# Another order for the 703 steps of a fused retention and channel-mix kernel

## Chip, cores and metric

The kernel runs on one core of a Trainium2 chip. The metric is the time of the device in microseconds (us), median of three runs. TensorE multiplies, VectorE (DVE in the rows), ScalarE (ACT) and GpSimd (POOL) work on whole tiles, SyncE (SP) starts most DMAs. PEld in the rows is TensorE loading weights, PE its multiplying.

## What is computed

Four sequences of 768 tokens go through a retention layer with 8 heads of 64 numbers (worked in blocks of 64 tokens with a state that is carried from block to block), and its output through a gated channel mix of width 512 and inner width 1024. All is f32.

```python
for b in range(nb):                      # blocks of 64 tokens
    intra = einsum(qb, kb) * Dmask       # decayed scores inside the block
    intra = einsum(intra, vb)
    inter = einsum(qb * lam_pow, kv_state)
    out[:, :, sl] = intra + inter
    kv_state = lam_block * kv_state + einsum(kb * rev_pow, vb)
x_prev = x shifted by one token
xk = mu_k * x + (1 - mu_k) * x_prev
xr = mu_r * x + (1 - mu_r) * x_prev
k = maximum(xk @ w_k, 0)
v = k * k @ w_v
return sigmoid(xr @ w_r) * v
```

## The kernel before

The tokens are worked in six rounds, n = 0 to 5, of 128 tokens (two blocks) of each sequence; the heads in four pairs, hp = 0 to 3. A round first does the retention of its four pairs, then the gate, then the two products of the channel mix. To keep f32 accuracy an f32 operand is split into a high and a low part (`split`, line 161: a copy on ScalarE, a subtraction on VectorE), and a product is three passes of matmuls, high by high, high by low, low by high (`product`, line 390).

What the kernel does is cut into steps of one letter and two digits; in most the first digit is the round. The step functions are:

- L, N, H (lines 104 to 118): loads by SyncE. S (176) loads a part of the weights; c (200), C (204) and D (221) turn it into high and low parts: a cast on ScalarE, a bit operation on VectorE, and a split. In these the letter r, k or v says of which weight.
- A `scores` (251), on TensorE: 16 small f32 matmuls for one head pair, which the trace records as 32. a `decay` (268), on VectorE, multiplies them by the decay mask. q (279) and k (283) scale queries on VectorE and keys on ScalarE, k with two instructions.
- U `sums` (289), on TensorE: 16 small matmuls (32 records) that give the two sums for a pair's state. u and w `next_state` (306), on VectorE from round 1 on: u makes the state after the first block from the sum, w the state after the second one from the sum and what u wrote. In round 0 u is a copy on ScalarE. Two pairs (0 and 1, 2 and 3) share the two PSUM tiles of the sums, each one half of both.
- B `values` (331) and G `values_too` (351), on TensorE, for two pairs at once: 16 and 48 small matmuls (32 and 96 records). g `turn` (348) copies one element on VectorE into a tile named junk, and so ties G to the end of B.
- e, E `mix_prev` (367): ScalarE scales the output of a pair, GpSimd moves the last column; f, F `mix` (374): VectorE adds the other term; y, x `split_x` (382): the split for the product. Small letters are for k, capitals for the gate in e and f.
- R, Q `r_part` (405): the gate's product, two of four output tiles each, 12 large matmuls from round 1 on; s (412) its sigmoid on ScalarE. K `k_part` (416): one of eight tiles of the first product, 12 large matmuls; h (422) squares its positive part (ScalarE, and VectorE from round 1 on), p (433) splits two tiles of it. V `v_part` (438): half of one tile of the second product, 12 large matmuls; o (460) multiplies by the gate on VectorE (the tile is called rt) and starts the DMA out from ScalarE's queue.
- Z `keep_busy` (156): matmuls on zeros at the start.

A step of TensorE that writes PSUM takes one of four buffers of the pool `ps_m` (tiles rp, kp, vp, xp), the one buffer of the scores, or the two of the sums. It waits until the readers of what was there are done.

The order of all steps is a table of text, `ORDER` (line 495), 703 steps long. The program calls them one after another (lines 472 to 477), and every engine keeps its own instructions in that order (`InOrder`, line 25). So an engine that waits in one step holds up all its later steps.

```python
for step in ORDER.split():
    ...
        i, j = step[1], int(step[2])
        steps[step[0]](i if i in "rkv" else int(i), j)
```

Of the kernel before, what the change touches and what calls it, by code (L numbers as in the profile page):

```python
# [492 lines left out]


ORDER = """
L01 M00 L00 Z10 d01 N01 A01 a01 H01 d02 H00 L02 k01 d00 A00 H02 U01 a00 N00 B01 L03 d03 A02 k00 u01 E01 l00 a02 H03
U00 k02 l02 u00 N02 B00 k03 N03 Sr0 A03 e00 E00 F01 U02 a03 Sr1 Sr2 U03 Sr3 Sk1 u02 u03 cr0 Sk0 e01 B03 E03 cr1 F00
B02 Cr0 f00 L11 Cr1 f01 cr2 L10 E02 R00 Cr2 F03 cr3 Q00 Q01 F02 y00 Dr2 N10 R01 Cr3 x02 e02 Q02 l01 N11 R02 x03 y01
Sk3 Dr3 Q03 N12 R03 f02 ck1 A10 ck0 e03 Ck0 L12 k11 k10 Ck1 f03 y02 Dk0 Dk1 U10 A11 U11 s00 y03 a10 s01 ck3 s02 Sk2
a11 q11 K03 h03 k12 u11 u10 q10 K01 h01 B10 g10 ck2 Sv1 Ck3 Sv0 Ck2 Dk3 A12 G10 s03 Dk2 N13 L13 cv1 K00 Sv3 a12 cv0  # L500
h00 w11 K02 h02 K07 Cv1 K06 l03 E10 Cv0 w10 e10 e11 Sv2 F10 U12 Dv0 E11 f11 f10 k13 p00 F11 p01 h07 A13 U13 q12 q13
K05 K04 cv3 Dv1 cv2 h05 Cv3 L21 a13 V00 Cv2 u13 h06 Dv3 N21 N23 h04 u12 Dv2 V02 B12 g12 A21 p02 y10 p03 G12 V01 x11
o00 x10 L20 e13 V03 y11 V04 e12 q21 N20 E12 o01 F12 f13 f12 a21 V06 V05 Dr0 o02 w12 y12 w13 L23 y13 V07 k20 A20 U20
K10 u20 E13 F13 K11 x12 a20 L22 k21 h10 K16 o03 Q10 x13 Q11 q20 h11 h16 Q12 Q13 U21 B20 A23 u21 N22 g20 A22 G20 p10
s12 k23 s13 N31 K17 h17 E21 K12 N30 q23 F21 e20 e21 a22 h12 p13 K14 f21 L30 k30 w21 K15 w20 E20 f20 h15 a23 h14 K13
k22 h13 F20 R10 x20 U23 L31 U22 B22 R11 u23 R12 g22 y21 u22 p11 q22 R13 G22 w22 o53 w23 A31 y20 A30 k31 q30 U30 E23
U31 s11 e23 e22 N33 s10 V10 a30 x21 E22 F23 L33 f22 F22 y22 f23 a31 V16 V14 p12 V17 u31 x23 V11 o10 V12 V15 x22 y23
u30 V13 o11 o12 N32 K27 o13 K26 Q20 Q21 h27 Q22 h26 Q23 p23 s22 q31 L32 B30 g30 A32 A33 G30 e31 s23 E30 f31 K24 K25
E31 e30 L41 F31 h24 K20 h20 N41 a33 q33 f30 w31 K23 w30 K21 h25 L40 F30 q32 K22 p22 h21 k32 R20 R21 k33 a32 h22 U33
k40 x30 h23 U32 y31 B32 N40 u32 R22 p20 R23 w32 y30 g32 u33 p21 G32 w33 A40 s20 A41 a41 k41 E32 U41 q41 F32 e33 e32  # L510
f33 x32 U40 q40 f32 V20 V21 u40 V22 a40 N43 N42 L42 o20 E33 s21 k42 y33 V23 B40 u41 y32 F33 g40 A42 w41 L43 x31 x33
A43 G40 o21 E41 E40 N50 Q30 e40 Q31 N51 a43 e41 F41 F40 f40 L50 Q32 Q33 s33 q42 K32 f41 V24 V25 s32 k43 K31 h32 V26
a42 K33 V27 h31 h33 K30 w40 L51 h30 K37 o22 k50 p31 R30 R31 q43 R32 R33 x40 o23 U42 h37 s31 U43 u42 u43 B42 g42 A50
A51 G42 s30 L52 q51 K34 K35 p30 h34 K36 a50 h35 E42 y41 y40 e42 a51 L53 h36 F42 e43 V32 V34 f42 f43 q50 x42 w42 p33
V30 p32 V31 y42 x41 y43 V35 o30 V33 E43 N52 o31 N53 V36 k52 V37 F43 K41 K42 o32 k51 w43 U50 x43 o33 u51 B50 g50 u50
A52 h41 A53 G50 h42 E51 a52 K43 e50 F51 h43 e51 K40 a53 E50 f50 K47 p41 F50 f51 K44 K45 h40 p40 h47 K46 h45 h46 R40
q52 R41 h44 k53 p42 R42 R43 B52 U52 u53 g52 s41 q53 s40 Q40 Q41 u52 Q42 Q43 G52 y51 s42 e53 y50 f53 s43 x50 e52 f52
p43 V42 V40 V41 x51 E52 E53 F53 o40 F52 y53 x52 y52 V43 K52 K53 V44 h53 K51 V45 o41 K54 o42 h52 V46 x53 h54 V47 p51
o43 K50 h51 Q50 K55 Q51 h50 h55 Q52 Q53 R50 s53 p50 K57 R51 s52 R52 h57 K56 h56 V52 R53 V50 p52 p53 V51 s50 V56 o50
s51 V53 V54 V55 o51 o52 V57  # L520
"""


# [60 lines left out]
```

## Time and profile before

| | before |
|---|---|
| median of 3 runs | 395.51 us (395.47 to 395.63) |
| span of the profiled execution | 393.7 us |
| TensorE multiplying | 386.9 us, 98% of the span |
| TensorE loading weights | 317.5 us |
| VectorE | 208.8 us |
| ScalarE | 168.5 us |
| GpSimd | 23.5 us |

The profile was taken in one execution, whose span runs from the first to the last instruction. All work is recorded through one helper, so every instruction stands at line 33 (L33), and groups are told apart by their tiles: `sc` the scores, `u` the sums, `st` the state, `mv` (in round 0 `mw`) the decayed scores, `xp` the output of the retention, `ts` the mix, `xh` and `xl` its two parts, `rp`, `kp` and `vp` the three products, `wst` a weight as it was loaded. TensorE's matmuls overlap one another, and their printed ends have the pipeline in them: what two rows tell of the time that one takes is the distance between their starts.

### The profile page before, as it was taken

Reading aid. Unit: us, or ns where it says so; the run is one execution under the profiler, and the core shown is the slowest. Engines: PE = TensorE matmul, PEld = TensorE weight load, DVE = VectorE, ACT = ScalarE, POOL = GpSimd, SP = SyncE. Lnnn points to the kernel's source line nnn. Section 1 sums busy time; section 2 is a strip of 40 time slices with the busy share of each in tenths; the row PEclk is TensorE's granted clock in tenths of the full one; section 3 lists DMA queues with packets and bytes.
Section 4 is the critical chain, followed back from the end, with each engine's and each line's share of the span. In section 5 each row is a group of like instructions: output and inputs, shape, how many; then the busy total and the mean of one; then the engine's idle time right before and its main releaser. Section 6 shows DMA issues by size and latency. Waiting matters only on the chain.

```text
span 393.7 us, 9414 instructions
## 1 busy us (share of the span) xinstructions
PE 386.9 (98%) x4154; PEld 317.5 (81%) x4154; DVE 208.8 (53%) x322; ACT 168.5 (43%) x276; POOL 23.5 (6%) x97
## 2 busy tenths in 40 slices
PE   7999999999999999999999999999999999999996
PEld 3757888888888888888888888888888888888885
DVE  4898989763377723358754026573373272232311
ACT  2798999443365412418353023542243360222300
POOL 2121010200001100100110000100000000000000
PEclk9999999999999999999999999999999999999999
DMA  7999861810320502230525001501000000000011
GB/s 265 412 407 412 305 246 55 303 45 28 116 102 11 208 27 82 81 136 2 200 68 219 0 27 42 203 19 64 28 2 1 3 27 27 28 27 0 2 42 65
DMA packets 15560, 42.64 MB, mean 108 GB/s; under 512 B 1440, under 2 KB 1824, under 8 KB 15520
## 3 DMA queue, kind: packets, MB, share of 16 engines
q1 hardware_dynamic: 11920, 35.76, 24.6%
q10 hardware_dynamic: 3600, 6.29, 4.4%
q8 instruction: 32, 0.52, 0.5%
q14 instruction: 8, 0.07, 0.1%
HBM read 35.76 MB, written 6.29 MB: 107 GB/s over the span
## 4 chain that ended last, share of the span: by engine, by line
PE 84%; ACT 8%; DMA 4%; DVE 1%; issue 1%; SPq 1%; POOL 0%; ACTq 0%; POOLq 0%
PE vp L33 32%; PE kp L33 29%; PE rp L33 14%; PE xp L33 4%; DMA wst<-w_r 2%; ACT kf L33 2%; ACT top L33 2%; PE u L33 2%; PE sc L33 2%; DMA in<-first 2%; ACT hiv L33 1%; ACT hik L33 1%; ACT ts L33 1%; SPq L33 1%; ACT xh L33 1%
## 5 line engine op out<-in xcount | busy, mean ns | idle before, releaser
L33 PE MATMUL vp<-hiv,k 128*128 128x512 f32 (+1 forms) x400 | 121.8, 382 | 0.0
L33 PEld LDWEIGHTS vp<-hiv,k 128*128 128x128 f32 x400 | 74.1, 188 | 14.6
L33 PE MATMUL vp<-lov,k 128*128 128x512 f32 (+1 forms) x200 | 76.1, 381 | 0.0
L33 PE MATMUL kp<-xh,hik 128*128 128x512 f32 x192 | 75.6, 394 | 0.3 <-ACT rt L33 0.3
L33 PE MATMUL kp<-xl,hik 128*128 128x512 f32 x192 | 74.8, 390 | 0.0
L33 PE MATMUL kp<-xh,lok 128*128 128x512 f32 x192 | 74.8, 390 | 0.0
L33 ACT ACTIVATE kf<-kp 128x512 f32<-128x512 f32 x48 | 28.3, 595 | 99.3 <-PE kp L33 84.1
L33 DVE TENSOR_TENSOR kf<-kp,kf 128x512 f32<-128x512 f32 x40 | 27.5, 690 | 67.7 <-ACT kf L33 67.6
L33 ACT ACTIVATE ts<-xp,omu 128x512 f32<-128x512 f32 x48 | 31.3, 687 | 29.8 <-DVE rt L33 12.1
L33 PEld LDWEIGHTS vp<-lov,k 128*128 128x128 f32 x200 | 37.6, 188 | 7.1
L33 PEld LDWEIGHTS kp<-xh,hik 128*128 128x128 f32 x192 | 36.0, 188 | 8.5 <-ACT rt L33 0.5
L33 PEld LDWEIGHTS kp<-xh,lok 128*128 128x128 f32 x192 | 36.0, 188 | 7.6
L33 PEld LDWEIGHTS kp<-xl,hik 128*128 128x128 f32 x192 | 36.0, 188 | 7.2
L33 DVE TENSOR_TENSOR xl<-ts,xh 128x512 fp32r<-128x512 f32 x46 | 30.9, 687 | 19.3 <-ACT xh L33 19.3
L33 DVE TENSOR_TENSOR rt<-vp,rt 128x512 f32<-128x512 f32 (+1 forms) x25 | 16.4, 666 | 45.4 <-PE vp L33 43.6
L33 ACT CAST xh<-ts 128x512 fp32r<-128x512 f32 x46 | 27.3, 617 | 25.2 <-DVE rt L33 20.3
L33 DVE SCALAR_TENSOR_TENSOR ts<-xp,mus,ts 128x512 f32<-128x512 f32 x46 | 33.4, 746 | 8.5 <-ACT ts L33 5.5
L33 DVE TENSOR_TENSOR k<-kf,k 128x1024 fp32r<-128x1024 f32 x24 | 29.2, 1222 | 13.0 <-ACT k L33 12.8
L33 PE MATMUL rp<-hir,xh 128*128 128x512 f32 x88 | 35.1, 399 | 0.0
L33 PE MATMUL rp<-hir,xl 128*128 128x512 f32 x88 | 34.3, 390 | 0.0
L33 PE MATMUL rp<-lor,xh 128*128 128x512 f32 x88 | 34.3, 389 | 0.0
L33 ACT CAST k<-kf 128x1024 fp32r<-128x1024 f32 x24 | 24.8, 1048 | 9.4 <-DVE kf L33 7.5
(58 smaller groups left out, 354.3 us busy)
## 6 DMA issues: line engine op xcount, KB each, us to landing
in<-kk SPq DMA_DIRECT2D x20, 512.0 KB, 6.4
in<-qv SPq DMA_DIRECT2D x20, 512.0 KB, 5.5
out<-rt ACTq DMA_DIRECT2D x23, 256.0 KB, 2.0
wst<-w_k SPq DMA_DIRECT2D x4, 1023.8 KB, 12.8
wst<-w_v SPq DMA_DIRECT2D x4, 1023.8 KB, 9.5
in<-first SPq DMA_DIRECT2D x4, 512.0 KB, 5.9
in<-first SPq DMA_DIRECT2D x8, 256.0 KB, 6.6
wst<-w_r SPq DMA_DIRECT2D x4, 511.8 KB, 8.8
```

Of the source, the lines that this page charges most:

```text
L33: return lambda *args, **kw: self.tc.keep_in_program_order(op(*args, **kw))
```

## The change

The 703 steps are the same ones, and no other line is touched. The table is written in another order from its first step to its last; some of its rows, of before and of after:

```diff
 ORDER = """
-L01 M00 L00 Z10 d01 N01 A01 a01 H01 d02 H00 L02 k01 d00 A00 H02 U01 a00 N00 B01 L03 d03 A02 k00 u01 E01 l00 a02 H03
-U00 k02 l02 u00 N02 B00 k03 N03 Sr0 A03 e00 E00 F01 U02 a03 Sr1 Sr2 U03 Sr3 Sk1 u02 u03 cr0 Sk0 e01 B03 E03 cr1 F00
...
-k22 h13 F20 R10 x20 U23 L31 U22 B22 R11 u23 R12 g22 y21 u22 p11 q22 R13 G22 w22 o53 w23 A31 y20 A30 k31 q30 U30 E23
...
+Z10 L01 N01 M00 d01 L00 A01 H01 l01 N02 a01 A00 H00 d00 k01 U01 L02 l02 N00 H03 L03 a00 k00 B01 E01 u01 d03 H02 A02 e01
+d02 k03 B00 a02 U00 u00 k02 f01 E00 N03 A03 Sr0 U02 U03 Sr1 F01 a03 B03 Sr2 F00 Sr3 Sk0 u02 u03 cr0 e00 Cr0 y01 E03 cr1
...
+Q10 o11 y21 V16 Q11 Q12 Q13 o10 w20 V17 x20 a22 U23 a23 u23 w23 A30 U22 u22 s13 B22 s12 g22 o13 A31 k31 G22 q31 e23 w22
+x21 L32 V14 e22 E23 V15 F23 x23 f23 E22 Q20 Q21 L33 F22 x22 f22 y22 Q22 y23 Q23 K21 s22 U30 N32 s23 a30 N33 h21 U31 u31
+K22 a31 w31 u30 B30 q30 g30 A32 h22 G30 w30 e30 k32 E30 e31 L41 A33 f30 a33 k33 o12 E31 K20 F30 k41 K25 q33 f31 F31 N41
+a32 R20 q32 N40 R21 h20 R22 R23 p20 x30 s20 x31 L40 U33 B32 s21 U32 u33 A40 u32 A41 g32 G32 K23 N43 h25 h23 q41 a41 K24
...
+V27 f32 y32 o22 o20 K30 q40 A43 B40 k43 U40 o23 g40 u40 U41 A42 u41 x33 G40 E40 K31 h30 K32 a42 x32 E41 h31 L51 h32 k42
...
```

Some places show what this does to single engines. The first is ScalarE at the start, in round 0: `in` are the scalings of keys (k, two rows for one step), `st` the copies u, `ts` the steps e and E, `top` the cast of the first weight part. Before:

```order
L33 ACTIVATE in<-in,Dw 128x4x64 x4
L33 COPY st<-u 128x256
L33 ACTIVATE ts<-xp,omu 128x4x128
L33 ACTIVATE in<-in,Dw 128x4x64 x2
L33 COPY st<-u 128x256
L33 ACTIVATE in<-in,Dw 128x4x64 x2
L33 ACTIVATE ts<-xp,omu 128x4x128 x2
L33 COPY st<-u 128x256 x2
L33 CAST top_100<-wst 128x512
```

After:

```order
L33 ACTIVATE in<-in,Dw 128x4x64 x4
L33 ACTIVATE ts<-xp,omu 128x4x128
L33 COPY st<-u 128x256
L33 ACTIVATE ts<-xp,omu 128x4x128
L33 ACTIVATE in<-in,Dw 128x4x64 x2
L33 COPY st<-u 128x256
L33 ACTIVATE in<-in,Dw 128x4x64 x2
L33 ACTIVATE ts<-xp,omu 128x4x128
L33 COPY st<-u 128x256 x2
L33 CAST top_100<-wst 128x512
```

Two more steps of mixing stand ahead of the cast where one stood in between, and one of them moved ahead of the copy.

The second is TensorE in round 2 where the sums of pairs 3 and 2 are made: U23 and U22 are 16 small matmuls each. Before, U23 is the first row of `u` here, U22 the next four, and B22 follows:

```order
L33 MATMUL rp<-hir_1091,xh_1013 128x512 [waits DVE_49]
L33 MATMUL rp<-lor_1093,xh_1013 128x512
L33 MATMUL rp<-hir_1091,xl_84 128x512
L33 MATMUL u<-in 64x64 x16
L33 MATMUL u<-in 64x64 [waits Activation_49]
L33 MATMUL u<-in 64x64
L33 MATMUL u<-in 64x64 [waits Activation_49]
L33 MATMUL u<-in 64x64 x13
L33 MATMUL xp<-mv,in 64x64 [waits DVE_49] x2
```

After, A30 (`sc`) stands between U23 and U22, B22 (`xp`) behind:

```order
L33 MATMUL vp<-hiv_989,k_3_993 128x512 x2
L33 MATMUL vp<-lov_990,k_3_993 128x512
L33 MATMUL vp<-hiv_989,k_3_993 128x512
L33 MATMUL u<-in 64x64 [waits DVE_49]
L33 MATMUL u<-in 64x64 x15
L33 MATMUL sc<-in 64x64 [waits DMAHW7_49,DMAHW5_49,DVE_49]
L33 MATMUL sc<-in 64x64 x15
L33 MATMUL u<-in 64x64 [waits DVE_49]
L33 MATMUL u<-in 64x64 x15
```

The matmul at the head of U22 now has a wait on VectorE.

The third is TensorE in round 4, where pair 0 and pair 1 get their sums. Before, U40 and U41 stand apart; here is U41, behind A42 and ahead of V:

```order
L33 MATMUL sc<-in 64x64 x15
L33 MATMUL sc<-in 64x64 [waits DMAHW2_49,DMAHW1_49]
L33 MATMUL sc<-in 64x64 x15
L33 MATMUL u<-in 64x64 [waits PE_49,Activation_49]
L33 MATMUL u<-in 64x64 [waits DVE_49]
L33 MATMUL u<-in 64x64 [waits Activation_49]
L33 MATMUL u<-in 64x64 x29
L33 MATMUL vp<-hiv_762,k_0_774 128x512
L33 MATMUL vp<-lov_763,k_0_774 128x512
```

After, U40 and U41 follow B40 at once, and A42 follows them:

```order
L33 MATMUL kp<-xh_481,hik_471 128x512
L33 MATMUL kp<-xl_83,hik_471 128x512
L33 MATMUL kp<-xh_481,lok_472 128x512
L33 MATMUL sc<-in 64x64 [waits DMAHW5_49,DMAHW0_49]
L33 MATMUL sc<-in 64x64 x15
L33 MATMUL xp<-mv,in 64x64 [waits DVE_49] x2
L33 MATMUL xp<-mv,in 64x64 x14
L33 MATMUL u<-in 64x64 x17
L33 MATMUL u<-in 64x64 [waits DVE_49]
L33 MATMUL u<-in 64x64 x14
L33 MATMUL sc<-in 64x64 [waits DMAHW7_49,DMAHW6_49]
```

The second matmul of U41 has a wait on VectorE.

The last is VectorE in round 3, around the step g30 (`junk`) that stands ahead of G30: `ts` are the steps f and F, `st` u and w, `mv` a, `rt` o. Before, the four rows of `rt` of round 1 stand earlier, and the rows are:

```order
L33 TENSOR_TENSOR rt<-vp,rt 128x512 [waits DMAHW2_49]
L33 TENSOR_TENSOR kf<-kp,kf 128x512 [waits Activation_49] x2
L33 TENSOR_TENSOR k_3_945<-kf,k_3_945 128x2x512 [waits Activation_49]
L33 TENSOR_TENSOR in<-in,LP 128x512 [waits DMAHW5_49]
L33 COPY junk<-xp 64x1 [waits PE_49]
L33 SCALAR_TENSOR_TENSOR ts<-xp,mus,ts 128x4x128 [waits Activation_49,Pool_49] x2
L33 TENSOR_TENSOR kf<-kp,kf 128x512 [waits Activation_49]
L33 TENSOR_TENSOR kf<-kp,kf 128x512 [waits DVE_49,Activation_49]
L33 TENSOR_TENSOR mv<-sc,Dt 128x512
L33 TENSOR_TENSOR in<-in,LP 128x512 [waits DMAHW1_49]
L33 SCALAR_TENSOR_TENSOR ts<-xp,mus,ts 128x4x128 [waits Pool_49]
```

After:

```order
L33 SCALAR_TENSOR_TENSOR st<-st,LP,u 128x256 [waits DVE_49,PE_49]
L33 SCALAR_TENSOR_TENSOR st<-st,LP,u 128x256
L33 TENSOR_TENSOR in<-in,LP 128x512 [waits DMAHW5_49,DMAHW4_49]
L33 COPY junk<-xp 64x1 [waits PE_49]
L33 TENSOR_TENSOR kf<-kp,kf 128x512 [waits Activation_49]
L33 SCALAR_TENSOR_TENSOR st<-st,LP,u 128x256 [waits DVE_49,PE_49]
L33 SCALAR_TENSOR_TENSOR ts<-xp,mus,ts 128x4x128 [waits PE_49,Activation_49,Pool_49]
L33 TENSOR_TENSOR mv<-sc,Dt 128x512 [waits PE_49]
L33 TENSOR_TENSOR rt<-vp,rt 128x512 [waits DMAHW4_49]
L33 SCALAR_TENSOR_TENSOR ts<-xp,mus,ts 128x4x128 [waits Pool_49]
L33 TENSOR_TENSOR in<-in,LP 128x512 [waits DMAHW7_49]
```

A step o (`rt`) that frees a PSUM buffer, o12, now stands behind f30 (`ts`) and a33 (`mv`).

## Rows read from the trace of the kernel before

**Rows 1.** The page: its head, busy time by engine, and one DMA queue.

```profile
span 393.7 us, 9414 instructions
...
PE 386.9 (98%) x4154; PEld 317.5 (81%) x4154; DVE 208.8 (53%) x322; ACT 168.5 (43%) x276; POOL 23.5 (6%) x97
...
q8 instruction: 32, 0.52, 0.5%
```

**Rows 2.** Busy time by stretch, two stretches; the first line names the columns.

```profile
core 0: us, PE busy (x) PEld busy (x) DVE busy (x) ACT busy (x) POOL busy (x), PEclk, DMA share, GB/s
...
18.06:33.27 15.21, 14.87 (x169) 9.35 (x169) 14.42 (x23) 14.39 (x24) 4.05 (x10) 1.00 1.03 409
...
66.69:390.46 323.77, 323.75 (x3344) 270.13 (x3344) 152.90 (x233) 112.92 (x190) 14.92 (x64) 1.00 0.19 68
```

**Rows 3.** The chain that ended last: start, us, engine, tile, matmuls.

```profile
84.88 0.62 PE sc L33 x32
85.50 0.48 PE u L33 x32
85.98 8.43 PE kp L33 x36
...
163.58 16.55 PE kp L33 x72
...
242.04 0.93 PE sc L33 x64
...
252.80 21.76 PE vp L33 x96
```

**Rows 4.** Timeline of ScalarE, 11 to 17 us: start, us, operation, [idle before <-releaser].

```profile
11.17 0.69 ACT L33 ACTIVATE ts<-xp,omu 128x512 f32<-128x512 f32 x1 [0.57 <-PE xp L33]
11.76 0.90 ACT L33 ACTIVATE in<-in,Dw 128x256 f32<-128x256 f32 x2
...
15.96 0.65 ACT L33 COPY st<-u 128x256 f32<-128x256 f32 x2 [0.37 <-PE u L33]
16.49 0.79 ACT L33 CAST top<-wst 128x512 f16<-128x512 bf16 x1
```

**Rows 5.** Timeline of TensorE, with the same columns.

```profile
8.41 1.16 PE L33 MATMUL sc<-in 64*128 64x128 f32 x16 [1.44 <-DVE mw L33]
...
12.17 0.69 PE L33 MATMUL u<-in 128*64 128x64 f32 x16
12.68 1.05 PE L33 MATMUL xp<-mw,in 128*64 128x128 f32 x16
...
14.76 1.15 PE L33 MATMUL u<-in 128*64 128x64 f32 x32
...
18.06 7.36 PE L33 MATMUL rp<-wr,x 128*128 128x512 f32 x16 [0.31 <-DVE wr L33]
...
33.27 0.50 PE L33 MATMUL kp<-xh,hik 128*128 128x512 f32 x1 [0.33 <-ACT rt L33]
...
66.69 0.69 PE L33 MATMUL xp<-mv,in 64*64 64x64 f32 x32 [0.22 <-DVE junk L33]
```

**Rows 6.** Timelines of TensorE's weight loads, VectorE and ScalarE.

```profile
19.89 0.19 PEld L33 LDWEIGHTS rp<-wr,x 128*128 128x128 f32 x1 [0.24 <-issue]
20.87 0.30 PEld L33 LDWEIGHTS rp<-wr,x 128*128 128x128 f32 x2 [0.79 <-DVE ts L33]
...
66.47 0.16 DVE L33 COPY junk<-xp 64x1 f32<-64x1 f32 x1
...
86.02 0.48 DVE L33 SCALAR_TENSOR_TENSOR st<-st,LP,u 128x256 f32<-128x256 f32 x1 [0.39 <-PE u L33]
...
163.70 0.69 ACT L33 ACTIVATE ts<-xp,omu 128x512 f32<-128x512 f32 x1 [3.13 <-PE xp L33]
...
164.49 0.75 DVE L33 SCALAR_TENSOR_TENSOR ts<-xp,mus,ts 128x512 f32<-128x512 f32 x1 [3.02 <-ACT ts L33]
```

**Rows 7.** Groups of VectorE's instructions by shape: busy us, mean ns of one, idle before.

```profile
L33 DVE TENSOR_TENSOR rt<-vp,rt 128x512 f32<-128x512 f32 x23 | 15.6, 687 | 34.8 <-PE vp L33 33.0 <-ACT rt L33 1.8
...
L33 DVE TENSOR_TENSOR mv<-sc,Dt 128x512 f32<-128x512 f32 x20 | 13.6, 683 | 1.0 <-PE sc L33 0.9
```

More of the change, by code (lines that the diff above doesn't have):

```diff
@@ L495 @@
 ORDER = """
-L01 M00 L00 Z10 d01 N01 A01 a01 H01 d02 H00 L02 k01 d00 A00 H02 U01 a00 N00 B01 L03 d03 A02 k00 u01 E01 l00 a02 H03
-U00 k02 l02 u00 N02 B00 k03 N03 Sr0 A03 e00 E00 F01 U02 a03 Sr1 Sr2 U03 Sr3 Sk1 u02 u03 cr0 Sk0 e01 B03 E03 cr1 F00
-B02 Cr0 f00 L11 Cr1 f01 cr2 L10 E02 R00 Cr2 F03 cr3 Q00 Q01 F02 y00 Dr2 N10 R01 Cr3 x02 e02 Q02 l01 N11 R02 x03 y01
-Sk3 Dr3 Q03 N12 R03 f02 ck1 A10 ck0 e03 Ck0 L12 k11 k10 Ck1 f03 y02 Dk0 Dk1 U10 A11 U11 s00 y03 a10 s01 ck3 s02 Sk2
-a11 q11 K03 h03 k12 u11 u10 q10 K01 h01 B10 g10 ck2 Sv1 Ck3 Sv0 Ck2 Dk3 A12 G10 s03 Dk2 N13 L13 cv1 K00 Sv3 a12 cv0
@@ L501 @@
[L501 to L505, printed above, removed]
@@ L506 @@
-k22 h13 F20 R10 x20 U23 L31 U22 B22 R11 u23 R12 g22 y21 u22 p11 q22 R13 G22 w22 o53 w23 A31 y20 A30 k31 q30 U30 E23
[L507 to L520, printed above, removed]
+Z10 L01 N01 M00 d01 L00 A01 H01 l01 N02 a01 A00 H00 d00 k01 U01 L02 l02 N00 H03 L03 a00 k00 B01 E01 u01 d03 H02 A02 e01
@@ new lines @@
+d02 k03 B00 a02 U00 u00 k02 f01 E00 N03 A03 Sr0 U02 U03 Sr1 F01 a03 B03 Sr2 F00 Sr3 Sk0 u02 u03 cr0 e00 Cr0 y01 E03 cr1
+f00 B02 E02 F03 Cr1 L10 Sk1 N10 cr2 N11 F02 y00 Q00 cr3 Cr2 x02 Cr3 e03 Dr2 o53 R00 e02 x03 l00 Dr3 f03 Q01 f02 k10 R01
+R02 R03 Q02 ck0 Q03 U10 Ck0 ck1 A10 Ck1 L11 Dk0 y02 A11 Dk1 s02 k11 u10 y03 a11 Sk3 s01 a10 K03 q11 s00 s03 K01 L12 l03
+N12 ck3 B10 Ck3 q10 U11 k12 g10 A12 h03 u11 Sk2 G10 h01 K00 Sv0 ck2 Ck2 Dk3 cv0 Sv1 E11 L13 Dk2 K02 h00 e11 e10 Cv0 f11
+cv1 E10 F11 w10 a12 w11 k13 K07 Sv2 K04 Cv1 U12 h02 F10 N13 A13 U13 Dv0 L21 Dv1 f10 K05 cv2 p01 p00 q12 q13 h07 h04 u12
@@ new lines @@
+K06 V00 a13 u13 h05 B12 Cv2 p02 g12 Sv3 N21 cv3 Cv3 Dv2 A21 h06 G12 y10 V02 a21 Dv3 p03 y11 e13 e12 q21 V01 w12 L22 L20
+N23 V03 k21 N20 f12 w13 o00 V04 x11 V05 o01 x10 A20 f13 y12 y13 U21 k20 U20 E13 F13 o02 u20 N22 a20 q20 K15 k22 K14 E12
+F12 h14 x13 Dr0 L23 V06 V07 o03 K12 B20 g20 A22 A23 u21 G20 x12 h12 N30 q22 L31 h15 E20 F20 K16 q23 K17 p12 h16 w21 e20
+h17 p13 K10 h10 E21 e21 f20 K11 k23 f21 L30 h11 k30 p10 R10 R11 K13 h13 p11 N31 R12 y20 R13 V10 F21 s11 V11 s10 V12 V13
+Q10 o11 y21 V16 Q11 Q12 Q13 o10 w20 V17 x20 a22 U23 a23 u23 w23 A30 U22 u22 s13 B22 s12 g22 o13 A31 k31 G22 q31 e23 w22
@@ new lines @@
+x21 L32 V14 e22 E23 V15 F23 x23 f23 E22 Q20 Q21 L33 F22 x22 f22 y22 Q22 y23 Q23 K21 s22 U30 N32 s23 a30 N33 h21 U31 u31
+K22 a31 w31 u30 B30 q30 g30 A32 h22 G30 w30 e30 k32 E30 e31 L41 A33 f30 a33 k33 o12 E31 K20 F30 k41 K25 q33 f31 F31 N41
+a32 R20 q32 N40 R21 h20 R22 R23 p20 x30 s20 x31 L40 U33 B32 s21 U32 u33 A40 u32 A41 g32 G32 K23 N43 h25 h23 q41 a41 K24
+K26 k40 p21 h24 h26 p22 K27 y30 E32 h27 E33 p23 V20 F32 a40 e33 f33 V21 w32 L42 N42 F33 y31 w33 V24 V26 y33 e32 V25 L43
+V27 f32 y32 o22 o20 K30 q40 A43 B40 k43 U40 o23 g40 u40 U41 A42 u41 x33 G40 E40 K31 h30 K32 a42 x32 E41 h31 L51 h32 k42
@@ new lines @@
+a43 V22 e41 f41 V23 w41 k51 N50 w40 L50 q43 F41 o21 K33 R30 R31 R32 h33 p31 q42 R33 F40 K37 s31 e40 f40 Q30 h37 s30 N51
+Q31 x40 k50 p30 Q32 Q33 B42 U43 U42 g42 s33 A50 u42 s32 u43 A51 G42 E43 F43 x43 w42 K34 K35 h34 K36 h35 y41 h36 p32 V30
+V36 E42 N53 y40 p33 e43 V37 e42 q50 a51 f42 V31 f43 F42 L52 a50 y43 y42 K40 w43 x41 q51 N52 o30 k52 K41 h41 K44 o33 L53
+U50 u51 u50 A52 B50 A53 g50 k53 U52 G50 h44 V32 E50 u52 e51 V33 F50 h40 o31 f51 K47 a53 x42 E51 V34 F51 V35 p40 K45 h47
+o32 K46 h46 h45 p43 K43 e50 f50 Q40 Q41 h43 Q42 Q43 u53 p42 s43 R40 R41 K42 a52 s42 y51 R42 h42 R43 q53 p41 B52 s40 s41
@@ L521 @@
+V46 q52 g52 G52 y50 V47 e52 V44 o43 f52 e53 x50 E53 V40 F53 x53 f53 y53 V45 V41 y52 E52 o40 o42 V42 K54 h54 x51 K50 h50
+K55 V43 F52 o41 K52 h55 K53 p52 K51 K57 x52 h53 h52 Q50 h51 p51 K56 Q51 Q52 Q53 h57 h56 p50 p53 s53 V57 s52 R50 R51 R52
+V54 V55 o52 V50 V52 R53 V53 s51 o51 V51 s50 o50 V56
 """
```

## The prediction

> **What bounds the kernel now.** I read the page first, then the busy time by stretch, then the chain that ended last, then the timelines of single engines where TensorE waits. The page has TensorE busy for 98% of the span [rows 1]. The table of stretches says where the other 2% are: from 18.06 to 33.27 us TensorE is busy for 14.87 of 15.21 us, and from 66.69 to 390.46 us for 323.75 of 323.77 us [rows 2]. In the long part TensorE never waits, so no order can win anything there except by making TensorE's own stream shorter. What is left to win is small: the first 18 us, 0.34 us before K03, one wait before G12, and the cost of changing between small and large matmuls. Everything else in this change can only keep the time or lose some.
>
> The cost of such a change of size comes from the chain [rows 3]. A run of large matmuls takes 21.76 / 96 = 0.2267 us each, a run of small ones 0.93 / 64 = 0.0145 us each. Where 32 + 32 small ones stand between large ones, the three pieces take 0.62 + 0.48 + 8.43 = 9.53 us; at the two rates 64 small and 36 large would be 0.93 + 8.16 = 9.09 us. One group of small matmuls, going in and coming out, thus costs 0.44 us, of which 8.43 - 8.16 = 0.27 us lie behind it.
>
> **The change part by part.** The instructions are the same; only their order on each engine differs. I counted the groups of small steps (A, U, B, G) between large ones (R, Q, K, V) after the first R: 16 before, 15 now. Saved: 0.44 us.
>
> *The start.* R00 starts at 18.06 and waits for the first weight, which ScalarE's cast at 16.49 begins; that cast stands behind the copies u02 and u03 at 15.96, which wait for U02 and U03 on TensorE at 14.76 [rows 4, 5]. The change puts on ScalarE, ahead of the cast, the same instructions in another order: E01 at 11.17, then u01, e01, k03, u00, k02. From the rows: 11.17 + 0.59 + 0.31 + 0.59 + 0.90 = 13.56. Now u00 has to wait for U00, which has changed places with B00: from 12.17 on, TensorE does B00 first (1.05 us, of which 0.18 overlap the next) and U00 ends near 13.75 [rows 5]. The copy and k02 (0.35 and 0.90) end near 15.15, and U02 starts at 15.2 and not at 14.76. Lost: about 0.45 us at R00. Against it stand 0.34 us of waiting before K03 [rows 2, 5]: in the changed order K03 needs s02, and the pair of k11 scalings (0.90 us on ScalarE) now stands behind s02 and not ahead of it, so ScalarE is there earlier by more than the lost 0.45. A weight load at 20.87 that waits for f01 (0.79 idle before it, 0.24 before the one ahead [rows 6]) no longer does, since f01 and f00 come earlier; of these 0.55 us TensorE covers a part with the matmul under way, and I take 0.2. Together 0.45 - 0.34 - 0.2 = -0.1 us, with ends of -0.9 (the 0.45 covered, all 0.55 won) and +0.45 (neither wait goes).
>
> *G12.* At 66.69 G12 waits for a tiny copy on VectorE (g12), which stands behind two splits of V weights [rows 5, 6]. Usually a group starts 0.18 us before the end printed for the last one (12.68 against 12.17 + 0.69: the printed end has the pipeline in it); here 0.22 after it, so 0.40 us are lost. In the new order only two of the four splits stand ahead of g12, and TensorE has B12 and A21 to cover it. Saved: 0.40 us. What can be late next is V01, in the last rival.
>
> Then four places where the new order puts a TensorE step directly behind a round trip through another engine. In the stretch where they lie, the order before has no wait of TensorE at all [rows 2]. E is the printed end of the TensorE step that starts the trip; the next group's turn is E - 0.18.
>
> *U22.* The new order is U23, u23, w23, A30, U22. U22 writes the tile that w23 reads, so it waits for VectorE. VectorE starts 0.04 after E (86.02 against 85.98 [rows 3, 6]), needs 0.48 for u23 and 0.48 for w23, which reads what u23 wrote (0.05 between them, an estimate from the 0.06 to TensorE), and TensorE starts 0.06 after (66.69 against 66.47 + 0.16): E + 1.11. TensorE has only A30, 0.47: its turn is E + 0.29. Lost: 0.82 us. Queued behind U22 are B22, A31, G22 and all that follows.
>
> *U41.* The order is U40, u40, U41 with nothing between; the second matmul of U41 waits for u40. E + 0.04 + 0.48 + 0.06 = E + 0.58 against E - 0.15. Lost: 0.73 us.
>
> *K25.* K25 needs the PSUM buffer that o12 frees. o12 now stands on VectorE behind f30 and a33, f30 waits for E30 on ScalarE, and E30 stands behind e30 and the two scalings k32, all after G30. From [rows 3, 4, 6]: e30 starts E + 0.12 (163.70 against 163.58), 0.59 to the next; the scalings 0.81 (0.90 less the overlap, below); E30 0.69: E + 2.21. f30 0.10 later (164.49 against the end 164.39), then 0.66 to a33, 0.60 to o12, 0.69 for it and 0.05 to TensorE: E + 4.31; the VectorE durations are those of [rows 6, 7], less about 0.09 by which neighbours on an engine overlap (11.17 + 0.69 against 11.76 on ScalarE is 0.10). TensorE has A33 (0.47), the 0.27 of coming back to large matmuls, and K20 (12 x 0.2267 = 2.72): E + 3.28. Lost: 1.03 us. Behind it wait R20 to R23 and B32.
>
> *G32.* g32 now stands behind u33 and u32, which both wait for U32: E + 0.04 + 0.78 (two starts, 0.48 less the overlap each) + 0.16 + 0.06 = E + 1.04, against A40 and A41, E + 0.75. Lost: 0.29 us.
>
> A wait of the first kind is in the trace: at 8.41 TensorE's scores waited 1.44 us until VectorE had read the tile that they overwrite [rows 5]. [...]
>
> The sum, against the median 395.51 (the profiled execution has a span of 393.7 [rows 1], so 1.8 us lie around it, and I leave these as they are): - 0.44 - 0.1 - 0.40 + 0.82 + 0.73 + 1.03 + 0.29 = +1.93. **397.4 us**, 0.5% slower.
>
> The ends of the unknown costs: each of the four waits can be met already (0), or cost about 0.1 more for starting the pipeline again; the start has -0.9 to +0.45. All high: 395.5 - 0.84 + 2.87 + 0.4 + 0.45 = 398.4. The low end is where half of the four do not bite.
>
> **Rivals.**
> *TensorE is late at these places anyway (faster).* TensorE's stream comes in pieces: 0.52 MB in 32 packets for 4154 matmuls and their weight loads [rows 1], so 16 KB and about 260 instructions a piece. If it arrived late where steps are small, VectorE would be ready by then and the four waits would cost nothing, while the savings stay: 397.4 - 2.87 = 394.6 us. It decides from a lateness of 0.3 us at G32 to 1.0 us at K25. For it: small matmuls use up a piece of 260 instructions, 130 matmuls, in 130 x 0.0145 = 1.9 us, and groups of 256 small ones occur in both orders. Against it: in the order before these groups lie in the stretch where [rows 2] leave 0.02 us idle in 323.77. Chance 0.06.
> [...]
>
> *The two U waits do not bite (within 0.2%).* If U22 and U41 found their half free, 397.4 - 1.55 = 395.9 us. The order of waits speaks against it: both steps carry a wait on VectorE. Chance 0.11.
>
> *The start slips more (slower still).* ScalarE and VectorE are busy for 14.4 of the 15.2 us up to K03 [rows 2], so a late R00 may not be made good, and V01 follows V02 at once now where it needs the last k tile, which ScalarE and VectorE split just before (p03). With 0.45 us at the start (its high end) and 0.4 us, as at G12 before, at V01: about 398.4 us, from a split that is over 0.4 us behind. Chance 0.08.
>
> That the change does something else than reorder I leave out: the engines' rows are the same ones in another order.
>
> **How the numbers follow.** The forecast of 397.4 has 0.75. A measurement of this kernel tells about 0.2%, 0.8 us, from no change; the forecast and the last rival are above 396.3, the second is within, the first below 394.7. Faster 0.06, same 0.11, slower 0.83. The range, 396.0 to 398.5, reaches from half of the four waits to all ends high; what it leaves out is the first rival and most of the second.
>
> **What would show it.** In the trace after: TensorE waits of 0.7 to 1.1 us on VectorE's rt (K25), st (U22, U41) and 0.3 on junk (G32), between 130 and 215 us; none before G12; R00 near 18.5 and K03 near 32.7. If the four are missing or under 0.2 us each, the forecast is wrong; if R00 is at 18.06, the start is worth 0.45 more.

## The result, and the profile after

The kernel with the new order takes 400.16 us (median of 6 runs, 398.52 to 401.18) against 395.59 us before (6 runs, 395.47 to 396.09): ratio 1.011, 95% interval 1.009 to 1.013. It is slower, as forecast, but by 4.6 us and not by 1.9, outside the stated range. Its runs differ by 2.7 us, and their time goes with the mean clock that TensorE was granted: 0.991 of full in the runs of 401.18 and 401.14 us, 0.996 in those of 400.41, 399.91 and 399.55, and 0.999 in that of 398.52 us. The profiled execution is the one of 401.18 us.

The page after, its head and the engines, which answer to [rows 1]:

```profile
span 399.4 us, 9424 instructions
...
PE 389.9 (98%) x4154; PEld 320.5 (80%) x4154; DVE 209.6 (52%) x322; ACT 170.1 (43%) x276; POOL 23.8 (6%) x97
```

The span grew by 5.7 us. TensorE's busy time grew by 3.0 us, though it has the same 4154 matmuls: where the granted clock was 0.50, the 16 matmuls of A00 took 2.08 us, and 1.16 before (below). What TensorE waited for, from the table of its waits (us in total, times, longest):

```profile
PE sc L33 <- DVE mw L33: 2.5, 1, 2.5
PE u L33 <- DVE st L33: 1.2, 2, 0.7
PE idle L33 <- DVE zeros L33: 1.2, 1, 1.2
PE kp L33 <- DVE rt L33: 0.8, 1, 0.8
PE rp L33 <- DVE wr L33: 0.3, 1, 0.3
PE xp L33 <- DVE junk L33: 0.3, 1, 0.3
```

The four waits of the forecast are all there, and with the releasers that it named: two on st (U22, U41), one on rt (K25), one on junk (G32). The first line is the one that was missed: before A00 TensorE waits 2.5 us, where the order before had 1.44 us [rows 5].

R00 and the last group of matmuls cut the span in two. From the chain after:

```profile
21.75 12.63 PE rp L33 x40
...
387.81 8.32 PE vp L33 x48
```

From R00 to the end of the last matmul it is 387.81 + 8.32 - 21.75 = 374.38 us. In the chain of the kernel before, the last piece is this:

```profile
371.07 19.38 PE vp L33 x108
```

With R00 at 18.06 [rows 5] that is 371.07 + 19.38 - 18.06 = 372.39 us. So the part behind R00 lost 1.99 us (forecast: 1.93 less the 0.45 that was priced for R00, 1.48), and R00 itself came 3.69 us later (forecast: 0.45), both in the profiled executions.

**The start.** SyncE's queue, after (start, us from the first issue to the last, what is loaded, how many):

```profile
0.73 0.87 SPq L33 DMA_DIRECT2D in<-first  x2
1.65 0.42 SPq L33 DMA_DIRECT2D smalls<-small  x1
2.12 6.93 SPq L33 DMA_DIRECT2D in<-first  x10
```

and before:

```profile
0.73 0.39 SPq L33 DMA_DIRECT2D in<-first  x1
1.18 0.42 SPq L33 DMA_DIRECT2D smalls<-small  x1
1.65 6.92 SPq L33 DMA_DIRECT2D in<-first  x11
```

M00, the load of the parameters (smalls), stands third and not second, behind N01. It is issued 0.47 us later (1.65 against 1.18), but the scans that wait for it start 2.1 us later (6.48 against 4.39): it is a load of 106 KB, now behind N01's 256 KB, and takes 4.8 us from issue to landing and not 3.2. VectorE after and, in the second fence, before (timelines: start, us, operation, idle time before):

```profile
6.48 0.74 DVE L33 TENSOR_TENSOR_SCAN Dw<-smalls 128x128 f32<-128x128 f32 x2 [4.28 <-DMA smalls<-small]
7.14 0.44 DVE L33 TENSOR_TENSOR_SCAN Dt<-smalls 128x64 f32<-128x64 f32 x2
7.50 0.26 DVE L33 TENSOR_TENSOR_SCAN LP<-smalls,zeros 128x64 f32<-128x64 f32 x1
7.69 1.26 DVE L33 TENSOR_TENSOR mw<-sc,Dw 128x512 f32<-128x512 f32 x2
```

```profile
4.39 0.74 DVE L33 TENSOR_TENSOR_SCAN Dw<-smalls 128x128 f32<-128x128 f32 x2 [2.18 <-DMA smalls<-small]
7.01 1.29 DVE L33 TENSOR_TENSOR mw<-sc,Dw 128x512 f32<-128x512 f32 x2 [1.89 <-PE sc L33]
```

Before, the scans were done long before a01 could start, which waited for TensorE. After, a01 waits for the scans, and behind those of d01 stand the three of l01 too. So a01 starts at 7.69 and not at 7.01, and A00, which writes the tile that a01 reads, at 9.05 and not at 8.41. TensorE, after:

```profile
5.37 1.16 PE L33 MATMUL sc<-in 64*128 64x128 f32 x16
9.05 2.08 PE L33 MATMUL sc<-in 64*128 64x128 f32 x16 [2.52 <-DVE mw L33]
```

A00 takes 2.08 us where A01 took 1.16. The table of stretches of 2 us shows the clock that was granted meanwhile (us from:to, their length, busy time of each engine, and at the end of a line granted clock, DMA share and GB/s):

```profile
6.00:8.00 2.00, 0.53 (x10) 0.34 (x7) 1.52 (x6) 0.00 (x0) 0.79 (x3) 1.00 0.97 378
8.00:10.00 2.00, 0.95 (x8) 0.98 (x10) 2.00 (x7) 0.91 (x2) 0.00 (x0) 0.63 1.06 419
10.00:12.00 2.00, 2.00 (x30) 1.78 (x28) 0.97 (x3) 0.91 (x2) 0.00 (x0) 0.50 1.04 400
12.00:14.00 2.00, 2.00 (x22) 1.67 (x20) 1.73 (x5) 0.00 (x1) 0.00 (x0) 0.50 1.03 394
14.00:16.00 2.00, 2.00 (x23) 1.88 (x24) 0.26 (x1) 2.00 (x5) 0.63 (x4) 0.66 1.06 414
```

Read the third number from the right. TensorE was busy for 0.53 and 0.95 us of the two stretches around its wait; within the second of them the granted clock falls from 1.00 to 0.50 (at 8.5 us), and it is back at 1.00 only after 15 us. Before, all stretches show 1.00, those around the wait of 1.44 us before A00 too:

```profile
6.00:8.00 2.00, 0.96 (x16) 0.77 (x14) 0.99 (x2) 0.00 (x0) 0.00 (x0) 1.00 0.92 322
8.00:10.00 2.00, 1.59 (x32) 1.50 (x34) 1.90 (x6) 1.61 (x4) 0.00 (x0) 1.00 1.02 397
```

### The profile page after: what moved, and what is told of

Read it like the earlier page. It is cut to its first block, busy times and chain, and to the rows that moved or that the text cites. A ratio compares the mean times of both kernels' runs of the same rounds, so it can differ in the third digit from the quotient of the medians.

```text
span 399.4 us, 9424 instructions
## 1 busy us (share of the span) xinstructions
PE 389.9 (98%) x4154; PEld 320.5 (80%) x4154; DVE 209.6 (52%) x322; ACT 170.1 (43%) x276; POOL 23.8 (6%) x97
## 4 chain that ended last, share of the span: by engine, by line
PE 95%; DVE 2%; DMA 1%; ACT 1%; issue 0%; SPq 0%; DVEq 0%
PE vp L33 33%; PE kp L33 33%; PE rp L33 17%; PE xp L33 6%; PE u L33 3%; PE sc L33 3%; DMA smalls<-small 1%; DVE st L33 1%; DVE mw L33 0%; DVE rt L33 0%; ACT in L33 0%; SPq L33 0%; DVE ts L33 0%; DVE Dw L33 0%; DVE wr L33 0%
## 5 line engine op out<-in xcount | busy, mean ns | idle before, releaser
L33 ACT ACTIVATE ts<-xp,omu 128x512 f32<-128x512 f32 x48 | 32.4, 688 | 33.0 <-PE xp L33 22.6
L33 ACT ACTIVATE rt<-rp 128x512 f32<-128x512 f32 x24 | 13.5, 594 | 37.7 <-PE rp L33 31.1
```

The source lines that it names most:

```text
L33: return lambda *args, **kw: self.tc.keep_in_program_order(op(*args, **kw))
```

## Experiments

Theory 1: the late parameters stop TensorE before A00, the clock falls in that stop, and with the four waits that is all. Theory 2: what I had priced in the front (the order on ScalarE, B00 ahead of U00) is what delays R00, and the clock falls anyway. A third question is the rival of the prediction: do the pieces in which TensorE's instructions arrive (32 packets [rows 1]) play a part? In each run below the kernel before was timed beside it, at 395.63 to 395.68 us (17 runs each time).

**M00 alone.**

```diff
-Z10 L01 N01 M00 d01
+Z10 L01 M00 N01 d01
```

> The new order with one step moved: M00 (the load of the parameters) back to the second place on SyncE, ahead of N01. Theory 1 (the parameters land late, A00 waits 2.5 us for the mask of pair 1, and TensorE's granted clock falls in that wait): the wait before A00 is near 1.4 us as before, A00 starts near 8.4 us, the granted clock stays 1.00, R00 starts near 18.5 us (before 18.06, new order 21.75) and the time is 397.5 to 398.2 us in every run, with little spread. Theory 2 (the order on ScalarE and the exchange of B00 and U00 delay R00, and the clock falls anyway): R00 stays above 20 us and the time near 400 us.

Measured: 399.44 us (4 runs, 399.26 to 400.71). The parameters landed as before, at 4.35 us, but A00 still waited, now for its own keys, since L00 stands behind N01 too. One cause was gone and the next one stood behind it: A00 started at 8.61 us, 0.44 earlier than in the new order. From the table of waits:

```profile
PE sc L33 <- DMA in<-first: 1.9, 1, 1.9
```

The clock fell in 2 of 4 runs (I count a run with a mean of 0.996 or less). The profiled one has R00 at 19.99 us. Neither theory had this wait in it. The two runs with a full clock took 399.26 and 399.46 us, no less than the one run of the new order that had a full clock (398.52 us): something besides the clock costs time here, and it was not found.

**l01 alone.**

```diff
-A01 H01 l01 N02 a01 A00
+A01 H01 N02 a01 l01 A00
```

> The new order with l01 (three scans on VectorE, 0.5 us) moved from ahead of a01 to behind it; M00 stays late. If late parameters are the larger part, A00 starts near 8.6 us, 0.45 earlier than in the new order, and the wait before it is near 2.0 us. Theory 1 says that the clock falls less or not at all: time 397.9 to 399.5 us. If l01 has no part in it, A00 stays at 9.05 us and the time near 400 us.

Measured: 399.23 us (4 runs, 398.83 to 400.3), about 0.9 us under the new order and inside what Theory 1 gave. That it is faster than the new order is not shown, since the intervals of the two ratios to the order before overlap (1.0069 to 1.0110 here, 1.009 to 1.013 there). The start that I expected for A00 did not come: the parameters landed at 6.88 us in the profiled run, 0.4 later than in the other, and A00 started at 9.12. The clock was down in 2 of 4 runs. The trace has one small wait that the new order's has not, 0.19 us at 278.70 us; its kind comes up again in the run with work in the wait.

**The two causes put into the order before.**

```diff
-L01 M00 L00 Z10 d01 N01 A01 a01
+L01 N01 M00 L00 Z10 d01 A01 l01 a01
```

(l01 is taken from its old place.)

> The order before, with only the two causes put in: M00 behind N01 on SyncE, and l01 ahead of a01 on VectorE. Theory 1: A00 starts near 9.05 us, the granted clock falls as in the new order, R00 starts between 18.7 us (no fall) and 21.3 us (a long one), and the time is 396.2 to 398.8 us with a spread like that of the new order. Theory 2: the order before is kept on ScalarE and TensorE, so the time is within 0.7 us of 395.5 us and the clock stays 1.00.

Measured: 396.49 us (12 runs, 395.50 to 399.32), ratio 1.0027 (1.0007 to 1.0048). The wait before A00 is 2.28 us, and the clock fell in 7 of 12 runs; in the two runs of 399.32 us its mean is 0.991. Two stretches of the profiled run:

```profile
8.00:10.00 2.00, 1.28 (x12) 1.31 (x14) 1.90 (x6) 1.24 (x3) 0.00 (x0) 0.58 1.03 409
10.00:12.00 2.00, 2.00 (x30) 1.77 (x30) 1.16 (x2) 0.63 (x3) 0.00 (x0) 0.56 1.06 420
```

This order has nothing else of the new one. So these two moves are enough to bring the fall of the clock, in 7 of 12 runs against 1 of 17 of the order before beside them, and Theory 2, by which this order keeps its clock, falls. Whether it is TensorE's idleness in the wait that brings it is asked below. The five runs with a clock of 0.999 to 1.000 lie at 395.5 to 396.2 us, from 0.2 us below the order before to 0.6 above it: without the clock, late parameters cost little in that order.

**The front of the new order alone**: its steps up to R00, then all others in the order before.

> The new order's steps up to R00, and behind them the order before for all other steps. Theory 1: TensorE waits 2.5 us before A00, R00 starts 1 to 3.7 us later than in the order before, by how long the clock is down; time 396.0 to 399.0 us, with a spread of 2 us or more, and none of the four waits (U22, U41, K25, G32). Rival (the front costs only the 0.45 us that I had priced): 395.3 to 396.2 us with little spread.

Measured: 398.09 us (6 runs, 397.83 to 398.57), ratio 1.0059 (1.0047 to 1.0071). The front alone costs 2.4 us here, but not in the way that I said: the clock was down in 3 of 6 runs and the time hardly differs. The waits tell why:

```profile
PE sc L33 <- DVE mw L33: 3.0, 1, 3.0
PE kp L33 <- ACT rt L33: 1.3, 1, 1.3
```

The new front puts other steps ahead of R00 than the old one does; the old rest, behind it, then has ScalarE late at K03: 1.27 us of waiting in the profiled run, whose clock was full, where the order before has 0.33. That the runs with a lower clock lose their time in the same wait is likely, but their traces are not kept. In the profiled run it is 10.40 us from A00 (9.17) to R00 (19.57) at a full clock. The mixture is a worse kernel than either part, and its 2.4 us are no measure of the front.

**Work in the wait.** Five more matmuls on zeros, in the wait.

```diff
-A01 H01 l01 N02 a01 A00
+A01 H01 l01 N02 a01 Z05 A00
```

> The new order with five matmuls on zeros (Z05, 0.43 us each, 2.1 us in all) added between A01 and A00, into the wait. A00 still starts near 9.05 us. Theory 1: the granted clock stays 1.00, so the steps from A00 to R00 run at full rate and R00 starts near 19.1 us instead of 21.75; time near 398.5 us in every run. Rival (the clock falls for another reason than TensorE's idleness there): the granted clock is 0.5 for some us all the same, time near 400 us and spread over 2 us.

Measured: 400.30 us (4 runs, 400.03 to 400.73), and the clock at 0.999 or 1.000 in all four: all stretches to 18 us show 1.00. A00 starts at 9.05 as in the new order, R00 at 19.45, and 0.58 us of that is another wait (for the first weight, 0.89 idle where the new order has 0.31). So the same steps take 10.40 - 0.58 = 9.82 us from A00 to R00 at full clock and 21.75 - 9.05 = 12.70 us in the profiled run of the new order: by this run the clock cost 2.9 us there. By the front alone, which took 10.40 us for the same steps at full clock and had no late weight, it cost 2.3 us. But the time did not fall, since two waits came up that the new order does not have:

```profile
PE kp L33 <- issue: 0.9, 1, 0.9
...
PE vp L33 <- issue: 0.5, 1, 0.5
```

"issue" means that nothing in the trace released TensorE. In its timeline:

```profile
217.07 0.50 PE L33 MATMUL kp<-xh,hik 128*128 128x512 f32 x1
218.52 0.39 PE L33 MATMUL kp<-xl,hik 128*128 128x512 f32 x1 [0.95 <-issue]
```

This one stands behind the first large matmul, and the other, at 145.45 us, behind the third, after a group of 256 small ones. Counted over all instructions of TensorE in the trace, in the order of their starts, the one at 145.45 is number 3521 and this one number 5569: 2048, or 8 x 256, apart (to within one, as some start together). Less these two waits and the late weight (0.51 + 0.95 + 0.58 us) the time would be near 398.3 us, an estimate from this run's own rows, which is where Theory 1 had it.

**The same zeros, without a longer stream.** Six zeros at the start and four in the wait, so that there are ten as in the new order.

```diff
-Z10 L01 N01
+Z06 L01 N01
...
-A01 H01 l01 N02 a01 A00
+A01 H01 l01 N02 a01 Z04 A00
```

> The new order with six of its ten matmuls on zeros at the start and four in the wait between A01 and A00. TensorE's stream has as many instructions as the new order has, so the pieces in which it arrives end where they do there; with the five added ones they ended ten instructions earlier in the work, and two waits for instructions came up (0.95 us each, at 145 and 218 us). If the place of the pieces makes these waits: none here, granted clock 1.00, R00 near 19.4 us, time 398.3 to 398.9 us. If the zeros themselves make them (the stop of the clock, or a longer stream of any place): they are here too, 399.5 to 400.5 us.

Measured: 399.91 us (6 runs, 398.54 to 401.56). No wait on issue in the trace: with a stream as long as in the new order the two (0.51 and 0.95 us, not 0.95 each) are gone, as the first part of the expectation has it. The two runs with a full clock, 398.54 and 398.92 us, fit that: they lie 1.6 us under the median of the run before, whose two waits come to 1.46. The other part missed, and the median lies in the range that I had given to the other case: four zeros take 1.04 us and not 1.7, a wait of 2.56 us was left before A00, and the clock fell in 4 of 6 runs, to 0.50 from 10 to 14 us:

```profile
PE sc L33 <- DVE mw L33: 2.6, 1, 2.6
```

**The front mended**: SyncE's order as before (M00 and L00 ahead of N01, L02 and H02 early), l01 behind a01, U00 ahead of B00.

```diff
-L01 N01 M00 d01 L00 A01 H01 l01 N02 a01 A00 H00 d00 k01 U01 L02 l02 N00 H03 L03 a00 k00 B01 E01 u01 d03 H02 A02 e01
-d02 k03 B00 a02 U00 u00 k02 f01 E00 N03
+L01 M00 L00 d01 N01 A01 H01 a01 A00 H00 d00 k01 U01 L02 l01 H02 N00 L03 a00 k00 B01 E01 u01 l02 d03 H03 A02 e01
+d02 N02 U00 u00 k02 B00 a02 k03 f01 E00 N03
```

> The new order with its front mended: on SyncE M00 and L00 ahead of N01, L02 and H02 early as in the order before; l01 behind a01; U00, u00 and k02 ahead of B00, k03 behind. From Sr0 on nothing is changed. Theory 1 (late parameters and late keys stop TensorE, and the stop costs it its clock): the wait before A00 is near 1.4 us, the granted clock stays 1.00, R00 starts near 18.1 us and all runs lie within 0.7 us of each other, as in the order before. What is left is what the rest of the order does: four waits of 3.3 us in all less savings of 1.4: 397.4 us (397.0 to 397.9). Rival (the rest is as wrong as the front): above 398.5 us.

Measured: 398.63 us (6 runs, 398.36 to 400.13), ratio 1.0077 (1.0061 to 1.0092); the clock was down in 1 of 6 runs. The wait before A00 is 1.44 us. R00 is at 19.05 us and not at 18.1: A00 came 0.43 later than before, and A03 waited 0.48 us for a02, which now stood behind seven scans on VectorE since a00, where the order before has five. The rest takes as long as in the new order: 374.54 us from R00 to the end of the last matmul, and 374.37 there. So the time lies where the rival had it, but 0.95 of the 1.23 us above my 397.4 are the front once more.

**The front mended once more**, with d02, l01 and l02 on VectorE where they stood before.

```diff
-a01 A00 H00 d00 k01 U01 L02 l01 H02 N00 L03 a00 k00 B01 E01 u01 l02 d03 H03 A02 e01 d02 N02 U00 u00 k02 B00 a02 k03
+a01 A00 H00 d02 d00 k01 U01 L02 H02 N00 L03 a00 k00 B01 E01 u01 d03 H03 l01 A02 e01 a02 N02 U00 u00 k02 l02 B00 k03
```

> The mended front again, with VectorE's steps also in the order that they had before (d02 behind a01, l01 behind d03, l02 behind a02), since A03 had waited 0.48 us for a02 behind five scans in the first mended front. The rest is the new order. If the front is what the prediction missed, and nothing else: R00 starts at 18.1 to 18.6 us and the time is 397.4 to 398.1 us, which is the forecast of 397.4 us with the restart of the pipeline at the four waits (0.45 us) added. If something else in the new order is slow: above 398.4 us, as with the first mended front.

Measured: 398.64 us (6 runs, 398.25 to 399.05), with the clock full in all six. Better in spread, no better in the median, and above the 398.4 us that were to tell of something else. In the trace that is the front again, since from R00 to the end of the last matmul it is 374.56 us, near the 374.37 of the new order. A03 no longer waits, but in the profiled run L00 landed late (A00 waits 1.6 us for it), and the first weight as well (R00 at 19.42 us, 1.0 idle before it). What VectorE no longer delays, the loads do; the DMA share is 0.97 to 1.07 from 6 to 22 us of that run.

**The four places mended**, on the first mended front.

```diff
-a22 U23 a23 u23 w23 A30 U22 u22 s13 B22 s12 g22 o13 A31 k31 G22
+a22 a23 U23 U22 u23 s13 B22 u22 s12 g22 A30 o13 A31 k31 G22 w23
...
-U33 B32 s21 U32 u33 A40 u32 A41 g32 G32
+U33 U32 u33 B32 s21 u32 g32 A40 A41 G32
...
-w30 e30 k32 E30 e31 L41 A33 f30 a33 k33 o12 E31 K20 F30 k41 K25
+w30 o12 e30 E30 L41 A33 f30 k32 F30 a33 e31 k33 E31 K20 k41 K25
...
-A43 B40 k43 U40 o23 g40 u40 U41 A42 u41 x33 G40
+o23 U40 U41 u40 B40 k43 u41 g40 A43 A42 x33 G40
```

> The order with the mended front, and the four places of the long part mended: U22 ahead of u23 and w23 (and A30 behind g22), U40 and U41 ahead of u40 (and A43 behind g40), o12 ahead of e30 and E30 ahead of k32, U32 ahead of u33. If the four waits are what they seem (3.3 us in all with the new start of the pipeline behind each): 394.1 us (393.8 to 394.6), faster than before. If a late piece of TensorE's instructions takes the place of a wait that is gone: 0.5 to 1 us at each place, 394.6 to 396.5 us, and the trace shows waits for no releaser there.

Measured: 395.65 us (12 runs, 395.07 to 397.26), ratio 1.0001 (0.9987 to 1.0014). The four waits are gone, and one new line stands in the table:

```profile
PE u L33 <- issue: 0.2, 1, 0.2
```

It is at 275.64 us, instruction 6849 of TensorE: 5 x 256 behind the second one above, and the place at which l01 alone had its 0.19 us. So this wait takes 0.24 us of the gain here; most of what is missing to 394.1 us is the front, which had missed its own forecast by 1.23 us. The clock was down in 3 of 12 runs, in the profiled one too, and there it fell when TensorE had long been at work again: A00 starts at 8.79 us, and the clock is still full to 10 us.

```profile
8.00:10.00 2.00, 1.21 (x17) 1.11 (x18) 1.89 (x8) 0.67 (x2) 0.00 (x0) 1.00 1.03 402
10.00:12.00 2.00, 1.93 (x25) 1.79 (x27) 2.00 (x6) 1.04 (x3) 0.00 (x0) 0.58 1.05 415
```

**Both together.** The second front, and the four places.

> The same front, and the four places mended as in the run with the first mended front. Waits of 2.7 us from R00 to the end gone, and one wait for TensorE's instructions near 273 us, 0.4 to 0.6 us, left: 394.7 to 395.2 us, faster than the order before by 0.1 to 0.25%. If the front is late again (A01 or A03): 395.4 us or more.

Measured: 395.21 us (12 runs, 394.90 to 396.30), ratio to the order before 0.9986 (0.9976 to 0.9997), clock full in all twelve. It is the fastest of the three orders (before, new, and this one), by 0.14%: little, but clear. The wait for TensorE's instructions that I expected near 273 us did not come. Its waits, all of them:

```profile
PE sc L33 <- DMA in<-first: 1.8, 1, 1.8
PE idle L33 <- DVE zeros L33: 1.2, 1, 1.2
PE u L33 <- ACT in L33: 0.6, 1, 0.6
```

The two runs with this front differ by the four places alone: 398.64 - 395.21 = 3.43 us. The two with the first mended front differ by 398.63 - 395.65 = 2.98 us. Not all of the 3.43 is the four places: in the two traces R00 starts at 19.42 and at 18.58 us, though the steps ahead of it are the same, because the first weight landed later in one (its cast waited 0.98 us for it there, and not at all in the other). From R00 to the end of the last matmul it is 374.56 and 371.51 us: 3.05 us for the four waits, with what goes with them.

## Why the prediction was wrong

**Right, but for the size of the savings: the part behind R00.** The chain after shows the waits one by one. U22:

```profile
141.44 0.69 PE u L33 x32
142.13 0.47 DVE st L33
...
142.70 0.49 DVE st L33
...
143.23 0.69 PE u L33 x32
```

U23, then u23 and w23 on VectorE, then U22: from the end of U23's piece at 142.13 to U22 it is 1.10 us, where the forecast had 1.11. U41 and G32 have the same form. TensorE's timeline at the three, with the idle time before each:

```profile
143.23 0.69 PE L33 MATMUL u<-in 64*64 64x64 f32 x32 [0.70 <-DVE st L33]
...
182.15 0.69 PE L33 MATMUL xp<-mv,in 64*64 64x64 f32 x32 [0.26 <-DVE junk L33]
...
216.08 0.63 PE L33 MATMUL u<-in 64*64 64x64 f32 x27 [0.50 <-DVE st L33]
```

K25, in the chain:

```profile
165.29 1.52 PE xp L33 x96
...
167.38 0.90 ACT in L33 x2
168.28 0.59 ACT ts L33
...
168.94 0.75 DVE ts L33
169.70 0.60 DVE mv L33
170.29 0.61 DVE rt L33
...
170.95 3.01 PE kp L33 x12
```

G30, then the two scalings, E30, f30, a33 and o12, as the forecast laid them out; from the end of G30 to K25 4.14 us, against 4.31. By the measure of the prediction (idle time plus the overlap that a group without a wait would have, 0.18 for small ones, as in the prediction, and 0.16 for large ones, printed with 0.39 us and 0.23 from start to start) U22, U41, K25 (0.79 idle) and G32 cost 0.70 + 0.18, 0.50 + 0.18, 0.79 + 0.16 and 0.26 + 0.18: 2.95 us in all, against 2.87. The traces of the run pair above give 3.05, so that 0.10 more goes with them. No row and no run shows the 0.4 for starting the pipeline again, which the prediction had as an end and not in the sum, nor the 0.45 that later expectations add for it. The four savings came too: no wait at f01, K03 or G12, and one group of small matmuls less. But their sum, 1.38 us, was too high: with the four waits gone, the part behind R00 takes 371.51 us against 372.39 before, 0.88 less. 2.95 - 0.88 = 2.07 us, and 1.99 were measured, 0.5 more than the forecast's 1.48. Which of the four fell short was not worked out. The rival of the two U waits (0.82 + 0.73 = 1.55 us) is answered as well: U22 and U41 wait, 0.70 and 0.50 us on st, though only the other half of the tile is read. That is as the order of waits had it; whether the chip needs that wait was not tried.

**Wrong: the term of the start**, -0.1 with ends of -0.9 and +0.45. It measured 3.69 us for R00 in the profiled run. The prediction took what lies ahead of 11.17 us as unchanged, and it priced a wait by its length alone. Three things were in the 3.69:
- A00, 0.64 us. The prediction followed ScalarE's and TensorE's orders from 11.17 us on and took what lay before as it was. It did not look at SyncE's queue, where M00 had changed places with N01, nor at VectorE's first rows, where l01 stood ahead of a01. Both are in the first line of the table. That step is the one that failed: every queue that a step is moved past counts, SyncE's too.
- U00 behind B00, priced at 0.45: 9.82 us (work in the wait) or 10.40 us (the front alone) from A00 to R00 at full clock against 18.06 - 8.41 = 9.65 before: 0.17 to 0.75 us, about what was priced.
- The clock, 2.3 to 2.9 us in the profiled run and the largest of the three. The prediction had no term for it. The stretches of before show 1.00 [rows 2], and those with its wait of 1.44 us before A00 [rows 5] show it too; that a longer one could have a second price was not asked.

The runs of the new order tell what the clock has in the median. At 0.991 of full they take 401.16 us on average (two runs), at 0.996 399.96 (three), at 0.999 398.52 (one). So of the 4.57 us of the median about 1.6 are the clock, and 2.93 are left at a full clock, by that one run; the late A00 (0.64), U00 (0.17 to 0.75) and the part behind R00 (1.99) come to 2.8 to 3.4 us. With the savings at f01 and K03 taken off, the end of +0.45 would have had to be 3.69 - 0.54 = 3.2.

**The rival of the pieces** (394.6 us, 0.06) did not happen here, since all four waits are there in full. But other orders have waits that no instruction in the trace ends: there are four on issue in three of them (0.51 and 0.95 us with five more zeros, 0.19 with l01 alone, 0.24 with the four places mended), at instructions 3521, 5569 and twice 6849 of TensorE. These are 2048 and 1280 apart, so all lie on one grid of 256 instructions (8 and 5 steps of it), and the 32 packets [rows 1] come to (4154 + 4154) / 32 = 260 instructions each. That these waits are late pieces is my reading of that grid; no row names what ended them. The two large ones are gone with the grid moved back by ten. The two small ones, both at instruction 6849, came with the grid where the new order has it, which shows no such wait there. What the prediction held against the rival, 0.02 us idle in the 323.77 where such groups lie [rows 2], was measured for the order before and does not carry over to every order: that one has groups as dense, and that the ends of its pieces lie in better places is a guess that was not tried on it.

**What stays open.** The clock fell in 21 of 34 runs of kernels whose profiled wait before A00 is 2.3 us or longer (the new order 5 of 6, l01 alone 2 of 4, the order before with the two causes 7 of 12, six and four zeros 4 of 6, the front alone 3 of 6), in 6 of 44 with a wait of 1.4 to 1.9 us, and in 2 of 51 of the order before. So the fall goes with a longer wait, and the wait does not decide it; the front alone had 3.0 us of wait in its profiled run and a full clock. Nor does the clock always fall inside the wait. In the profiled runs, by stretches of half a microsecond, it did so in the new order (8.5 us), with l01 alone (9.0), in the order before with the two causes (8.3) and with six and four zeros (8.9), but with M00 alone it fell 0.5 us after A00 had started, and with the four places mended 1.5 us after. That work in the wait kept the clock up rests on four runs, and 1.78 us of the wait were left in the profiled one. What else decides was not found.

## What to carry to other kernels

When a table of steps is reordered, go through every queue from its first entry, the load queue first: a small load that moves behind a larger one can land much later than its issue moved (2.1 us against 0.47 here), and what hangs on it can be the whole front. A wait of TensorE early in a kernel may cost more than its length (here the 2.5 us before A00 went with a granted clock of 0.50, which cost another 2.3 to 2.9 us in the profiled run), so look at the granted clock around it and not only at busy time. A round trip through another engine can be priced well from neighbouring rows: the four came out within 0.05 to 0.15 us of the forecast each, and undoing them gave back what they had cost.
